# A random-feature attention with a feed-forward part: weight loads in turns of five, a key chunk's two loads asked for together, the second tile's attention behind a gate

## The chip, the cores and the metric

The kernel runs on one core of a Trainium2 chip. Its time is the device time of one execution in microseconds (us). The engines are PE (TensorE), DVE (VectorE), ACT (ScalarE), POOL (GpSimd) and SP (SyncE), which here issues all the transfers. "Before" is the kernel as it was, "after" the one with the change.

## The reference

```python
# q, k, v: (8, 8, 576, 64); omega: (128, 64); x: (8, 576, 512); w_ch1: (512, 2048); w_ch2: (2048, 512)
def phi(x):
    proj = np.einsum('bhsd,md->bhsm', x, omega)
    sq = np.sum(x * x, axis=-1, keepdims=True) / 2.0
    h = proj - sq
    h = h - np.max(h, axis=-1, keepdims=True)
    return np.exp(h) / np.sqrt(m)
q_p, k_p = phi(q * scale), phi(k * scale)
kv = np.einsum('bhsm,bhsd->bhmd', k_p, v)
z = np.sum(k_p, axis=2)
num = np.einsum('bhsm,bhmd->bhsd', q_p, kv)
den = np.einsum('bhsm,bhm->bhs', q_p, z)[..., None] + 1e-06
x = (num / den) with the heads side by side
xn = (x - mean) / np.sqrt(var + 1e-06) * g_ln
out = x + np.maximum(xn @ w_ch1, 0.0) @ w_ch2
```

Everything is 32-bit. A batch's `kv` needs all 576 of its keys, so no query of a batch gets its numerator before the batch's last key chunk is through.

## The kernel before, in words

**Stages.** Attention goes by key chunks and query blocks. A batch has five key chunks (four of 128 rows, one of 64): keys and values are loaded (L372, L376), projected on PE (L439), reduced to row maxima on DVE (L395), put through the exponential on ACT (L401), multiplied with the values on PE (L418), and added up in `kv` on DVE (L424). A query block has 256 rows, loaded in two parts (L465), projected (L494), copied out of PSUM by ACT or DVE (L229, L231), reduced over partitions on POOL (L478), subtracted on DVE (L480) and exponentiated on ACT (L483). For each 128 rows `gen_x` multiplies with `kv` (L555), divides, and takes the norm's statistics; `gen_xnT` normalizes and transposes (L624, L628, L630) into `xnT`, of which there is one.

The feed-forward part takes the 4608 rows as nine tiles of 512. A tile has 16 steps f. A step is `mm1` (L651 to L653, twelve matmuls of 128x512), a relu on ACT and DVE (L662, L664) and `mm2` (L684 to L686, twelve matmuls). A tile begins when its four transposed chunks and the first four w1 parts are there.

**Weights.** Each of w1 and w2 comes in 16 parts of 512 KB as 64-bit words that hold doubles. `gen_w` loads a part (L314) into a tile of its own and turns it, by six operations on ACT and DVE (L321 to L354), into two 32-bit parts in place, the rounded value and the rest. At most three are converted at once (`turn_w`). `mm1` at step f needs w1 parts up to the end of f's group of four, `mm2` needs w2 part f. The converted weights stay for the whole kernel.

**The order of the work.** Every piece is a Python generator that asks a planner for names (`get`: a tile, a PSUM bank, or a mere turn that stands for no memory), for engine time (`run`, with an assumed cost) or for another piece's result (`wait`). The planner simulates the engines with its assumed costs and emits instructions in the order that comes out: among what could start first on an engine, the lowest rank goes. That order is fixed in the program; on the chip each engine, SP too, takes its instructions in order and waits for data by semaphores. Ranks: a batch's keys start at `NS * (b * S // T) + RK`, a block's queries at `NS * (blk * QB // T) + RQ + 4 * (blk % 2)`, with NS = 32, RK = -30, RQ = -22, so -30 and -22 for the first tile and 2 and 10 for the second; weights at `RW0 + RW * f` (w1) and one more (w2), from -12 and -11 to 18 and 19; the feed-forward part comes behind all of them on PE, and its relu ahead of all of them on ACT and DVE. While no feed-forward matmul has started, `gen_warm` fills PE's planned idle time with small matmuls (L709), whose result is not used.

Names of which there are few: 15 wide tiles for raw keys, queries, query features, conversions and normalized rows (`wide`, N_BIG); two key turns; two query turns; two blocks at once; three value tiles.

In `gen_keys` the values of a chunk are asked for when its keys have landed, by the planner's clock, and the next chunk's keys when the values have:

```python
                yield dma(P * NP * r)
                nc.sync.dma_start(kraw, kT[b, c] if c < NFULL else kTr[b])
                t_v = yield "get", n_v
                v = tile_of(t_v, [P, H, D + 1])
                yield dma(P * H * D)
                nc.sync.dma_start(v[0:r], vF[b, c] if c < NFULL else vR[b])
```

Of the kernel before, what the change touches and what calls it, by code (L numbers as in the profile page):

```python
# [12 lines left out]
F32 = mybir.dt.float32  # L13
BF16 = mybir.dt.bfloat16
F32R = mybir.dt.float32r
U32 = mybir.dt.uint32
# [6 lines left out]
P = 128  # L23
B, H, S, D = 8, 8, 576, 64
M = 128
DM = H * D
DFF = 4 * DM
NP = H // 2
NK = DM // P
NF = DFF // P  # L30
NFULL = S // P
# [4 lines left out]
T = 512  # L36
# [3 lines left out]
QB = 256  # L40
# [28 lines left out]
class Plan:  # L69
# [73 lines left out]
    def free(self, *names):  # L143
        for n in names:
            assert n not in self.places, n
            self.places[n] = self.cur.seen()
            self.cur.holds -= n[0] == "b" and 0 < self.cur.holds
            self.wake(lambda w: w[0] == "get" and n in w[1])

    def done(self, key):  # L150
        self.made[key] = self.cur.seen()
        self.wake(lambda w: w == ("wait", key))
# [38 lines left out]
def favor_ffn(ctx, tc, kT, kTr, vF, vR, qT, omT, gT, w1, w2, out):  # L191
# [12 lines left out]
    nc = tc.nc  # L204
    const = ctx.enter_context(tc.tile_pool(name="const", bufs=1))
    wp = ctx.enter_context(tc.tile_pool(name="wp", bufs=1))
    sb = ctx.enter_context(tc.tile_pool(name="sb", bufs=1))
    ps = ctx.enter_context(tc.tile_pool(name="ps", bufs=1, space=PSUM))
    plan = Plan()
    free, done = plan.free, plan.done  # L210

    def f32(ap):
        return ap.bitcast(F32)
# [4 lines left out]
    def dve(n, k=1, c=0.065):  # L218
        return "run", {DVE: k * (c + 0.00105 * n)}
# [4 lines left out]
    def dma(n):  # L224
        return "run", {SP: n * 4e-6 / 0.36}

    def copy(eng, out, in_):
        if eng == ACT:
            nc.scalar.copy(out=out, in_=in_)  # L229
        else:  # L230
            nc.vector.tensor_copy(out, in_)  # L231

    def scaled(eng, out, in_, c):
        if eng == ACT:
            nc.scalar.activation(out=out, in_=in_, func=AF.Copy, scale=c)
        else:
            nc.vector.tensor_scalar(out=out, in0=in_, scalar1=c, scalar2=None, op0=ALU.mult)

    def wait(*key):
        return "wait", key  # L240

    def names(tag, n):
        return plan.own(*(f"{tag}{i}" for i in range(n)))

    def tile_of(tag, shape, dtype=F32, pool=sb):
        return pool.tile(shape, dtype, tag=tag, name=tag, bufs=1)

    def bank(tag, n=512):
        return tile_of(tag, [P, 512], F32, ps)[:, 0:n]


    n_big, n_x, n_kp, n_v, n_kv = names("wide", N_BIG), names("x", 9), names("kp", 2), names("v", 3), names("kv", 3)
    n_hid, n_xnT, n_mb, n_st = names("hid", 2), names("xnT", 1), names("mb", 3), names("st", 9)
    turn = {k: names(f"turn_{k}", n) for k, n in (("k", 2), ("q", 2), ("blk", 2), ("mx", 2), ("xn", 4), ("w", 3))}
    n_w = {(n, f): names(f"w{n}_{f}", 1) for f in range(NF) for n in (1, 2)}
    banks = names("b", 8)
    b_at, b_h, b_acc = banks[0:2], banks[2:4], banks[4:8]
# [14 lines left out]
    nc.vector.memset(eps, EPS)  # L272
    g_sb = const.tile([P, NK], F32, name="g_sb")
    om_raw = tile_of("hid0", [P, M])
    if TILED:
        om = const.tile([P, M], F32, name="om")
# [31 lines left out]
    wparts = {}  # L308

    def gen_w(n, f):  # L310
        tag = yield "get", n_w[n, f]
        yield dma(2 * P * DM)
        r = tile_of(tag, [P, DM, 2], U32, wp)
        nc.sync.dma_start(r.rearrange("p a b -> p (a b)"), (w1, w2)[n - 1][f])  # L314
        w_turn = yield "get", turn["w"]
        wt = yield "get", n_big
        eng = yield "run", {ACT: 0.56, DVE: 0.34}
        t = tile_of(wt, [P, DM], U32)
        sign = 0x80000000
        if eng == ACT:  # L320
            nc.scalar.activation(out=t, in_=r[:, :, 0], func=AF.Copy, scale=2.0**-29 * 7.49 / 8)  # L321
            yield dve(DM)
            nc.vector.scalar_tensor_tensor(
                out=r[:, :, 0], in0=r[:, :, 1], scalar=sign, in1=t, op0=ALU.bitwise_and, op1=ALU.bitwise_or
            )
            eng = yield "run", {ACT: 0.56, DVE: 0.34}
            scaled(eng, f32(r[:, :, 1]), f32(r[:, :, 1]), 2.0**-112)
        else:
            nc.vector.tensor_scalar(out=t, in0=r[:, :, 1], scalar1=sign, scalar2=None, op0=ALU.bitwise_and)
            eng = yield "run", {ACT: 0.56, DVE: 0.34}  # L330
            scaled(eng, f32(r[:, :, 1]), f32(r[:, :, 1]), 2.0**-112)
            yield dve(DM)
            nc.vector.scalar_tensor_tensor(
                out=r[:, :, 0], in0=r[:, :, 0], scalar=29, in1=t, op0=ALU.logical_shift_right, op1=ALU.bitwise_or
            )
        yield dve(DM)
        nc.vector.scalar_tensor_tensor(  # L337
            out=t, in0=r[:, :, 1], scalar=3, in1=r[:, :, 0], op0=ALU.logical_shift_left, op1=ALU.bitwise_or
        )
        if n == 1:  # L340
            yield wait("g")
        eng = yield "run", {ACT: 0.56, DVE: 0.34}
        w = wparts[n, f] = tile_of(tag, [P, 2, DM], F32R, wp)
        if n == 1:
            g = g_sb[:, f % NK : f % NK + 1]
            scaled(eng, w[:, 0], f32(t), g)
            yield dve(DM)
            nc.vector.scalar_tensor_tensor(
                out=w[:, 1], in0=f32(t), scalar=g, in1=f32(w[:, 0]), op0=ALU.mult, op1=ALU.subtract
            )  # L350
        else:
            copy(eng, w[:, 0], f32(t))
            yield dve(DM)
            nc.vector.tensor_tensor(out=w[:, 1], in0=f32(t), in1=f32(w[:, 0]), op=ALU.subtract)  # L354
        free(wt, w_turn)
        done(("w", n, f))

    kvs, phis, xs, xnTs = {}, {}, {}, {}
# [1 line left out]

    def gen_keys():
        for b in range(B):
            t_kv = yield "get", n_kv
            kvs[b] = t_kv, tile_of(t_kv, [P, H, D + 1])
            for c in range(NFULL + 1):
                plan.cur.rank = NS * (b * S // T) + RK + 2 * c
                r = P if c < NFULL else REM
                k_turn = yield "get", turn["k"]
                t_k = yield "get", n_big
                kraw = tile_of(t_k, [P, NP, r])  # L370
                yield dma(P * NP * r)
                nc.sync.dma_start(kraw, kT[b, c] if c < NFULL else kTr[b])  # L372
                t_v = yield "get", n_v
                v = tile_of(t_v, [P, H, D + 1])
                yield dma(P * H * D)
                nc.sync.dma_start(v[0:r], vF[b, c] if c < NFULL else vR[b])  # L376
                t_kp = yield "get", n_kp
                t_mb = yield "get", n_mb
                plan.add(plan.cur.rank, gen_k(b, c, r, kraw, v, (t_k, k_turn), (t_kp, t_mb, t_v)))
# [131 lines left out]

    def gen_queries():
        for blk in range(NB):
            plan.cur.rank = NS * (blk * QB // T) + RQ + 4 * (blk % 2)
            b_turn = yield "get", turn["blk"]
            plan.add(plan.cur.rank, gen_block(blk, b_turn))

    def gen_block(blk, b_turn):
        rank = plan.cur.rank
        for j in range(2):  # L520
            plan.add(rank, gen_q(blk, j))
        for i in range(2):
            plan.add(rank + 6 + 2 * i, gen_x(2 * blk + i))
        for j in range(2):
            for s in range(2):
                yield wait("phi", blk, j, s)
        yield wait("num", 2 * blk)
        yield wait("num", 2 * blk + 1)
        free(*(phis[blk, j, s][0] for j in range(2) for s in range(2)), b_turn)
# [203 lines left out]
    NS = 2 * NF  # L733
    plan.add(-300, gen_const())
    for f in range(NF):
        plan.add(RW0 + RW * f, gen_w(1, f))
        plan.add(RW0 + RW * f + 1, gen_w(2, f))
    plan.add(RK, gen_keys())
    plan.add(RQ, gen_queries())
    plan.add(URGENT, gen_xnT())  # L740
    for b in range(B):
# [5 lines left out]

TILED = True
N_BIG = 15
WARM, COLD = 0.1, 5.0  # L750
RW0, RW = -12, 2
RK, RQ = -30, -22


# [32 lines left out]
```

## Time and profile before

| | |
|---|---|
| time, median of 3 runs | 1142.06 us (1141.39 to 1143.84) |
| the profiled execution: time, span | 1141.77 us, 1139.9 us |
| mean granted clock of PE | 0.974 |
| busy: PE, DVE, ACT, POOL | 1100.3, 484.8, 330.2, 131.2 us |
| moved by DMA | 55.70 MB |
| first feed-forward matmul (L651) starts | 132.07 us |
| weight loads (L314) | 32 of 512 KB, 2.6 to 42.4 us, median 9.4 us from issue to landing |

Busy time counts when an engine has an instruction under way. Matmuls are pipelined, so PE's filler matmuls and its useful ones both count as busy, and a busy PE is not PE at its peak. A row of a group reads: line, engine, operation, output and input, shapes and count, then busy time, mean length in ns, and the idle time ahead of it with what ended it. SPq is SP's queue, which issues transfers. Clock and DMA lines on the page stand for 40 equal slices of the span, in tenths.

### The profile page before, as it was taken

How to read it: one execution, taken by the hardware profiler on the slowest of the kernel's cores; microseconds unless marked ns; L12 is line 12 of the kernel's file. 1: busy time of each engine (PE TensorE's matmuls, PEld its weight loads, DVE VectorE, ACT ScalarE, POOL GpSimd, SP SyncE). 2: the span in 40 equal slices, each digit the busy share in tenths (PEclk: the TensorE clock that was granted, in tenths of full speed). 3: DMA queues.
4: the chain of work that ended last, by engine and by line, in shares of the span. 5: the costliest groups of instructions: out<-in, count | busy, mean ns of one | idle time of the engine just before them, and what ended most of it. 6: DMA issues, size and time to landing. Idle time of an engine off the chain costs nothing.

```text
span 1139.9 us, 15141 instructions
## 1 busy us (share of the span) xinstructions
PE 1100.3 (97%) x6135; PEld 902.2 (79%) x6135; DVE 484.8 (43%) x1074; ACT 330.2 (29%) x795; POOL 131.2 (12%) x77
## 2 busy tenths in 40 slices
PE   5669999999999999999999999999999999999998
PEld 3558888788788878887888788887887888888886
DVE  3997844534741373136422642164137116113111
ACT  3884623343331134113321242123113112111110
POOL 2200500400400050004000220013004000000000
PEclk8776999999999999999999999999999999999999
DMA  9802212012100120003100310020011000000000
GB/s 355 330 28 84 66 56 59 28 56 93 47 1 1 46 92 22 1 4 127 28 1 1 112 43 6 1 74 1 1 38 38 1 1 37 1 1 37 1 1 37
DMA packets 26340, 55.70 MB, mean 49 GB/s; under 512 B 3104, under 2 KB 4256, under 8 KB 26272
## 3 DMA queue, kind: packets, MB, share of 16 engines
q1 hardware_dynamic: 26272, 54.75, 13.9%
q8 instruction: 48, 0.79, 0.3%
q14 instruction: 20, 0.16, 0.0%
HBM read 45.30 MB, written 9.44 MB: 48 GB/s over the span
## 4 chain that ended last, share of the span: by engine, by line
PE 90%; DVE 5%; ACT 2%; DMA 1%; issue 1%; POOL 0%; SPq 0%; DVEq 0%
PE b L651 12%; PE b L684 12%; PE b L686 12%; PE b L685 12%; PE b L653 11%; PE b L652 11%; PE b L418 6%; PE b L555 6%; PE b L439 4%; PE b L494 3%; PE b L624 1%; DVE wide L337 1%; DMA w<-w 1%; DVE w L354 1%; ACT kp L401 1%
## 5 line engine op out<-in xcount | busy, mean ns | idle before, releaser
L664 DVE SCALAR_TENSOR_TENSOR hid<-b,hid 128x512 fp32r<-128x512 f32 x144 | 99.5, 691 | 464.4 <-ACT hid L662 464.2
L662 ACT ACTIVATE hid<-b 128x512 fp32r<-128x512 f32 x144 | 86.2, 599 | 519.5 <-PE b L653 519.3
L684 PE MATMUL b<-w,hid 128*128 128x512 f32 x576 | 233.7, 406 | 0.1
L651 PE MATMUL b<-xnT,w 128*128 128x512 f32 x576 | 232.9, 404 | 0.0
L686 PE MATMUL b<-w,hid 128*128 128x512 f32 x576 | 226.5, 393 | 0.0
L685 PE MATMUL b<-w,hid 128*128 128x512 f32 x576 | 226.0, 392 | 0.0
L653 PE MATMUL b<-xnT,w 128*128 128x512 f32 x576 | 225.2, 391 | 0.0
L652 PE MATMUL b<-xnT,w 128*128 128x512 f32 x576 | 224.7, 390 | 0.0
L478 POOL PARTITION_ALL_REDUCE wide<-wide x72 | 130.8, 1889 | 741.3 <-ACT wide L229 634.8
L651 PEld LDWEIGHTS b<-xnT,w 128*128 128x128 f32 x576 | 108.3, 188 | 29.4 <-issue 7.5
L684 PEld LDWEIGHTS b<-w,hid 128*128 128x128 f32 x576 | 108.2, 188 | 26.4 <-issue 3.0
L686 PEld LDWEIGHTS b<-w,hid 128*128 128x128 f32 x576 | 108.1, 188 | 24.6
L653 PEld LDWEIGHTS b<-xnT,w 128*128 128x128 f32 x576 | 108.1, 188 | 23.5
L685 PEld LDWEIGHTS b<-w,hid 128*128 128x128 f32 x576 | 108.4, 188 | 21.4
L652 PEld LDWEIGHTS b<-xnT,w 128*128 128x128 f32 x576 | 108.4, 188 | 20.0
L418 PE MATMUL b<-v,kp 128*128 128x65 f32 (+1 forms) x640 | 85.2, 284 | 30.6 <-ACT kp L401 30.2
L418 PEld LDWEIGHTS b<-v,kp 128*128 128x128 f32 (+1 forms) x640 | 83.7, 201 | 38.7 <-ACT kp L401 32.2
L401 ACT ACTIVATE kp<-b,mb 128x128 f32<-128x128 f32 (+1 forms) x320 | 87.5, 382 | 74.2 <-DVE mb L395 74.2
L555 PEld LDWEIGHTS b<-kv,wide 128*128 128x128 f32 (+1 forms) x640 | 72.9, 195 | 6.5 <-issue 2.6
L480 DVE TENSOR_TENSOR wide<-wide,wide 128x512 f32<-128x512 f32 x72 | 69.5, 976 | 18.1 <-POOL wide L478 18.0
L555 PE MATMUL b<-kv,wide 128*128 128x65 f32 (+1 forms) x640 | 72.5, 276 | 1.9 <-DVE st L561 1.7
L395 DVE TENSOR_REDUCE mb<-b 128x4 f32<-128x512 f32 (+1 forms) x80 | 51.8, 684 | 40.4 <-PE b L439 40.3
(51 smaller groups left out, 745.2 us busy)
## 6 DMA issues: line engine op xcount, KB each, us to landing
w<-w SPq DMA_DIRECT2D x32, 512.0 KB, 9.4
wide<-qT SPq DMA_DIRECT2D x36, 256.0 KB, 3.1
out<-x SPq DMA_DIRECT2D x36, 256.0 KB, 2.1
v<-vF SPq DMA_DIRECT2D x32, 260.0 KB, 2.9
wide<-kT SPq DMA_DIRECT2D x32, 256.0 KB, 2.9
v<-vR SPq DMA_DIRECT2D x8, 130.0 KB, 2.6
wide<-kTr SPq DMA_DIRECT2D x8, 128.0 KB, 2.6
hid<-omT SPq DMA_DIRECT2D x1, 64.0 KB, 1.8
```

Source lines behind the costliest of these rows:

```text
L401: nc.scalar.activation(out=kp[0:r, j], in_=pk[0:r, i], func=AF.Exp, scale=1.0, bias=mb[0:r, j : j + 1])
L418: nc.tensor.matmul(pv[:, i], kp[0:r, slot(h)], v[0:r, h], start=True, stop=True)
L478: nc.gpsimd.partition_all_reduce(mx, qc, P, bass_isa.ReduceOp.max)
L555: nc.tensor.matmul(pn[a:z, i], phi(blk, h, slice(cols + a, cols + z)), kvs[b][1][:, h], start=True, stop=True)
L651: nc.tensor.matmul(ph, w[:, 0, cs], xnT[:, 0, k], start=(k == 0), stop=False)
L652: nc.tensor.matmul(ph, w[:, 1, cs], xnT[:, 0, k], start=False, stop=False)
L653: nc.tensor.matmul(ph, w[:, 0, cs], xnT[:, 1, k], start=False, stop=(k == NK - 1))
L662: nc.scalar.activation(out=hl[:, 0], in_=ph, func=AF.Relu)
L664: nc.vector.scalar_tensor_tensor(out=hl[:, 1], in0=ph, scalar=0.0, in1=f32(hl[:, 0]), op0=ALU.max, op1=ALU.subtract)
L684: nc.tensor.matmul(accs[i], hl[:, 0, cs], w[:, 0], start=(f == 0), stop=False)
L685: nc.tensor.matmul(accs[i], hl[:, 0, cs], w[:, 1], start=False, stop=False)
L686: nc.tensor.matmul(accs[i], hl[:, 1, cs], w[:, 0], start=False, stop=(f == NF - 1))
```

## The change

Five edits, none of which changes what is computed or how much of it:

- A weight part must hold one of five load turns (`turn_wl`) from ahead of its load until it is converted.
- A key chunk's keys and values are asked for in one step of the planner, with the keys' size counted twice.
- The second batch's keys wait until w2 part 7 is converted, the third query block (the first of the second tile) until w2 part 8 is: that is nine parts of w2, 0 to 8.
- The weights' ranks become -14 + f for w1 and -5 + f for w2.
- `tile_of` picks the weights' pool by the tile's name, where `gen_w` named it.

```diff
-    turn = {k: names(f"turn_{k}", n) for k, n in (("k", 2), ("q", 2), ("blk", 2), ("mx", 2), ("xn", 4), ("w", 3))}
+    turn = {k: names(f"turn_{k}", n) for k, n in (("k", 2), ("q", 2), ("blk", 2), ("mx", 2), ("xn", 4), ("w", 3), ("wl", 5))}
...
-    def tile_of(tag, shape, dtype=F32, pool=sb):
+    def tile_of(tag, shape, dtype=F32, pool=None):
+        pool = pool or (wp if tag[1].isdigit() and tag[0] == "w" else sb)
...
     def gen_w(n, f):
+        load_turn = yield "get", turn["wl"]
         tag = yield "get", n_w[n, f]
         yield dma(2 * P * DM)
-        r = tile_of(tag, [P, DM, 2], U32, wp)
+        r = tile_of(tag, [P, DM, 2], U32)
...
-        free(wt, w_turn)
+        free(wt, w_turn, load_turn)
         done(("w", n, f))
...
     def gen_keys():
         for b in range(B):
+            if b == 1:
+                yield wait("w", 2, GATE_K)
...
-                yield dma(P * NP * r)
-                nc.sync.dma_start(kraw, kT[b, c] if c < NFULL else kTr[b])
                 t_v = yield "get", n_v
                 v = tile_of(t_v, [P, H, D + 1])
-                yield dma(P * H * D)
+                yield dma(2 * P * NP * r)
+                nc.sync.dma_start(kraw, kT[b, c] if c < NFULL else kTr[b])
                 nc.sync.dma_start(v[0:r], vF[b, c] if c < NFULL else vR[b])
...
     def gen_queries():
         for blk in range(NB):
+            if blk == T // QB:
+                yield wait("w", 2, GATE_Q)
...
-        plan.add(RW0 + RW * f, gen_w(1, f))
-        plan.add(RW0 + RW * f + 1, gen_w(2, f))
+        plan.add(RW1 + RS * f, gen_w(1, f))
+        plan.add(RW2 + RS * f, gen_w(2, f))
...
+GATE_K, GATE_Q = 7, 8
-RW0, RW = -12, 2
+RW1, RW2, RS = -14, -5, 1
```

More of the change, by code (lines that the diff above doesn't have):

```diff
@@ L342, in gen_w @@
         eng = yield "run", {ACT: 0.56, DVE: 0.34}
-        w = wparts[n, f] = tile_of(tag, [P, 2, DM], F32R, wp)
+        w = wparts[n, f] = tile_of(tag, [P, 2, DM], F32R)
         if n == 1:
```

## The prediction

> **What bounds the kernel now.** I read the page first, then a table of the span cut where the first matmul of the feed-forward part (L651) starts, then the order of events ahead of that point.
>
> ```profile
> span 1139.9 us, 15141 instructions
> ...
> DVE  3997844534741373136422642164137116113111
> ...
> PEclk8776999999999999999999999999999999999999
> DMA  9802212012100120003100310020011000000000
> ```
>
> DVE is full and PE's clock below full speed only in the first slices, and DMA is busy only there. The cut table (columns: PE, PEld, DVE, ACT, POOL busy with counts, granted clock, DMA share, GB/s):
>
> ```profile
> 0.00:132.07 132.07, 98.33 (x711) 82.27 (x711) 104.36 (x216) 82.46 (x177) 23.53 (x18) 0.78 0.48 180
> 132.07:1139.90 1007.83, 1001.97 (x5426) 819.91 (x5425) 380.45 (x859) 247.69 (x618) 107.71 (x60) 1.00 0.10 32
> ```
>
> From 132.07 us on PE works 1001.97 of 1007.83 us at full clock. Nothing but less PE work could shorten that stretch, and the change removes none. The first 132 us are different. PE's groups there, by line:
>
> ```profile
> L709 PE MATMUL b<-spin 128*128 128x256 bf16 x326 | 44.7, 298 | 1.2 <-DVE spin L265 1.2
> L418 PE MATMUL b<-v,kp 128*128 128x65 f32 (+1 forms) x112 | 19.8, 339 | 30.2 <-ACT kp L401 30.2
> ...
> L439 PE MATMUL b<-om,wide 64*128 64x128 f32 (+1 forms) x128 | 11.4, 328 | 0.0
> L494 PE MATMUL b<-wide,om 64*128 64x256 f32 x64 | 9.8, 429 | 2.0 <-DMA wide<-qT 2.0
> ```
>
> 44.7 us of "busy" is the warm-up filler of L709, which computes nothing, and 30.2 us are idle behind ACT's exponentials. So the bound is the start of the feed-forward part. What sets it is in the order of events (start, length, engine):
>
> ```profile
> 11.01 0.44 SPq L372 DMA_DIRECT2D wide<-kT  x1
> ...
> 12.20 16.26 SPq L314 DMA_DIRECT2D w<-w  x14
> ...
> 18.76 7.41 POOL L478 PARTITION_ALL_REDUCE wide<-wide  x4 [9.70 <-issue]
> 20.60 1.56 DVE L480 TENSOR_TENSOR wide<-wide,wide 128x512 f32<-128x512 f32 x1 [9.80 <-POOL wide L478]
> ...
> 29.35 0.33 SPq L376 DMA_DIRECT2D v<-vF  x1
> ...
> 30.59 12.11 SPq L314 DMA_DIRECT2D w<-w  x11
> ...
> 43.73 0.33 SPq L372 DMA_DIRECT2D wide<-kT  x1
> ...
> 44.55 1.16 PE L439 MATMUL b<-om,wide 64*128 64x128 f32 x16
> ...
> 73.18 1.16 PE L439 MATMUL b<-om,wide 64*128 64x128 f32 x16
> ...
> 86.91 2.08 PE L439 MATMUL b<-om,wide 64*128 64x128 f32 x16
> ...
> 94.02 1.09 PE L439 MATMUL b<-om,wide 64*64 64x128 f32 x16
> ```
>
> The second key chunk's keys are issued at 11.01, its values at 29.35, with weight loads between; the third chunk's keys at 43.73, behind the last weight load. The first batch's chunks 1 to 4 reach PE at 44.55, 73.18, 86.91 and 94.02. Only then can the first tile's numerators (L555) start, as the chain of waits shows (start, length):
>
> ```profile
> 101.17 13.92 PE b L555 x64
> 115.09 2.01 PE b L439 x16
> ...
> 117.64 1.40 PE b L439 x16
> ...
> 121.78 1.03 ACT kp L401 x4
> 122.90 1.03 ACT kp L401 x4
> ...
> 124.41 1.05 ACT kp L401 x4
> 125.50 2.00 PE b L418 x16
> ...
> 128.38 1.73 PE b L418 x16
> 130.12 1.09 PE b L439 x16
> 131.21 0.87 PE b L494 x8
> 132.07 0.43 PE b L651
> ...
> 132.75 0.23 PE b L653
> ```
>
> L439, L418, L401 and L494 after 115 us belong to the second tile: five first-batch chunks and two query blocks were already through. They sit ahead of the first tile's last transposes.
>
> **The change part by part.** *Key and value loads together.* Each chunk loses one serial wait, in which the values were asked for only after the keys had landed. SP issues the same DMAs; their place among the weight loads changes. *Five load turns.* `turn_wl` is a name in the planner and no tile, so the chip gets no new semaphore from it: it changes the emitted order. A load is put behind key loads that have become due, and the fourteen and eleven weight loads in a row disappear. A first-tile chunk should then meet a few weights ahead of it, not all 32. The pool choice in `tile_of` gives the same tiles: nothing. *Ranks.* w1 goes ahead of w2; the order from the ranks is five loads in order of asking (w1 0, w2 0, w1 1, w2 1, w1 2), then w1 3 to 10, and from there w2 2 and on alternating. *Gates.* The second batch's keys wait for w2 7, which by that order is about the 24th weight of 32, the third query block for w2 8, about the 25th. In the emitted order this moves L439, L418, L494 and all their ACT, DVE, POOL and SP instructions behind those conversions; behind the waiting generator only later batches are queued.
>
> *Where the start goes.* DVE cannot go on before 20.60, since the first all-reduce began at 18.76 after 9.70 us of issue; the change doesn't touch that, so I keep it. In a sentence that the sum doesn't use: the Trainium skill (GPSIMD Engine Reference, 2.1 Instruction dispatch) gives about 6 us for the first call of a freshly loaded routine; by it DVE would be let go 3.7 us sooner and the time would be 1090. The row's 9.70 is longer, and decides.
>
> From 20.60, chunk by chunk: with keys and values in time the shortest spacing seen is 94.02 - 86.91 = 7.1 us, and that with DVE full of conversions. Four more chunks make 28.4, the last kv add about 1 (an estimate): L555 starts at 50. From L555 to L651 took 132.07 - 101.17 = 30.9 us. The second tile's pieces quoted above (2.01 + 1.40 + 3.11 + 3.73 + 1.09 + 0.87 = 12.2) leave by the gate: 18.7. So the feed-forward part starts at **69 us** (20.6 + 28.4 + 1 + 18.7).
>
> The same from DVE's work, since DVE may be what is full:
>
> ```profile
> L337 DVE SCALAR_TENSOR_TENSOR wide<-w 128x512 uint32<-128x512 uint32 x32 | 22.5, 717 | 0.0
> L323 DVE SCALAR_TENSOR_TENSOR w<-w,wide 128x512 uint32<-128x512 uint32 x27 | 18.5, 694 | 0.5 <-ACT wide L321 0.5
> L348 DVE SCALAR_TENSOR_TENSOR w<-wide,g_sb,w 128x512 fp32r<-128x512 f32 x16 | 12.0, 749 | 0.0
> L354 DVE TENSOR_TENSOR w<-wide,w 128x512 fp32r<-128x512 f32 x16 | 11.9, 743 | 0.0
> ```
>
> These four groups are 64.9 us for 32 weights, 2.03 us of DVE each. DVE worked 104.36 us before 132.07, so some 39 us were attention; by the chunks and blocks that stay behind the gate about a quarter of that goes (an estimate), leaving 29. With N weights converted ahead of the start, it comes at 20.6 + 29 + 2.03 N. Ten weights give 70, in agreement; the six that are needed or asked first give 62, sixteen give 82. I take 69, with 50 (chunks at 2.5 us each: 20.6 + 10 + 1 + 18.7) and 85 (seventeen weights between) as ends.
>
> Clock: the chain's L555 took 13.92 us for 64, while the granted clock was about half:
>
> ```profile
> 100.00:110.00 10.00, 9.76 (x50) 9.39 (x49) 6.90 (x22) 2.46 (x5) 0.00 (x0) 0.56 0.25 69
> 110.00:120.00 10.00, 10.00 (x68) 8.86 (x68) 6.97 (x33) 0.87 (x5) 0.00 (x0) 0.59 0.20 65
> ```
>
> The same work in the changed kernel also follows gaps at ACT's exponentials, so I keep 13.92; at twice the clock it would be 7 us shorter, inside my lower end. The Trainium skill (TensorE: Matmul & The Clock Gate, Part 1) says full clock comes after about 3.4 us of sustained activity, which would end the half clock early in L555 and bring the time to about 1089. Here PE was busy 19.76 of 20 us and stayed near half, so this trace speaks against it.
>
> *What the later part gets back.* Ahead of 132.07 the old kernel had also done second-tile work: 128 - 80 = 48 records of L439 (three chunks), 112 - 80 = 32 of L418 (two chunks), 64 - 32 = 32 of L494 (four groups of 8). At full clock that is 3 x 1.09 + 2 x 1.73 + 4 x 0.87 = 10.2 us; each return to the feed-forward part costs 0.43 - 0.23 = 0.2, nine times 1.8. Sum 12.0 us, now behind the start.
>
> *New waits in the first tile.* Weights must now arrive while PE uses them. A step f is 24 matmuls at 0.23, 5.5 us; 16 steps are 88 us for the 22 weights left, 4.0 us each, against 2.03 of DVE. Where weights and relu (L662, L664) stand in a line on ACT and DVE, PE can still wait some tenths per step: 0 to 15 us, and I take 3, near the lower end because DVE needs only half of its time. Below nothing is excluded: no PE work disappears.
>
> **Sum.** 69 + 1007.8 + 12.0 + 3 = 1091.8 us of span. The profiled execution took 1141.77 for 1139.9 of span, 1.9 more: 1093.7, or **1094 us**. That execution is 0.3 below the median of 1142.06, too little to matter.
>
> **The rivals.** *Weights too late.* The start comes early, but PE waits for weights. For: they are now loaded and converted under the feed-forward part, with relu on the same two engines. Against: the 2.03 us. It decides when a weight takes more than 4.0 us; at 5 us each, 22 take 110 instead of 88, and the time is 1094 + 22 = 1116.
>
> *The second tile too late, the one that ends slower.* The gate holds the second batch's keys until about weight 24. PE has 88 us of steps and about 26 us of the second tile's attention (as the first tile's: 5 x 1.09 + 5 x 1.73 + 4 x 0.87, half of 13.92 for L555 and, an estimate, 2 for L624) until 69 + 88 + 26 = 183. At 2.5 us per weight (32 in the 80 us from 20 to 100) the gate opens at 69 + 14 x 2.5 = 104; five chunks at 7.1 and 31 us of the rest end at 171, in time. At the mean spacing of before, (94.02 - 44.55) / 3 = 16.5, they end at 104 + 82 + 31 = 217, a gap of 34 us and 1128. It turns the result slower once the second tile is ready after 183 + 48 = 231, that is a gate at 118 with the old spacing; at 4 us per weight it opens at 125, and the time is 1149.
>
> *The order doesn't really change.* The five turns bind only the planner, and DVE was full from 20 to 100 us. If nearly all 32 conversions still go ahead of the first tile's last steps, the start is 20.6 + 29 + 65 = 115, and 115 + 12 + 1007.8 + 3 + 1.9 gives 1140, no change. Against: the planner gives a free engine to the lowest rank that is ready, and the keys' ranks (-30 to -22) are below the weights'; it was the loads that were missing.
>
> **How the numbers follow.** Start between 55 and 85: 0.70. Earlier still: 0.07, about 1075. Weights late: 0.10. Second tile late enough to be slower: 0.08. Order unchanged: 0.05, of which 0.04 within 0.2% (2.3 us, about what a measurement of this kernel can tell from no change) and 0.01 faster. Faster is 0.70 + 0.07 + 0.10 + 0.01 = 0.88, same 0.04, slower 0.08. The low end is a start at 50 without new waits, 50 + 1007.8 + 12 + 1.9 = 1072; the high end a start at 85 with about 13 us of new waits, 1120. What lies outside is most of the slower case, the unchanged order and the tails.
>
> **What would show it.** In the profile after: the first batch's five key loads issued before about 30 us with weights between; the L439 rows of chunks 1 to 4 by 50; L651 first at 55 to 85 and far fewer L709 records than 326; the conversions (L337) running on beside L651; no second-batch L439 ahead of the first L651; and PE at 99% afterwards. A first L651 past 100, idle PE between L653 and L684 behind a weight's L354, or a gap of PE ahead of the second tile's first L651 would make it wrong, each by one of the rivals.

## The result, and the profile after

After the change the kernel takes 1111.7 us (median of 4 runs, 1108.05 to 1113.58) against 1141.72 for the kernel before: ratio 0.9733, 95% interval 0.970 to 0.9765. The gain is 30 us; 48 was forecast, with a range of 1072 to 1120. The profiled execution took 1110.21 us for a span of 1108.4.

The page of the kernel after, the lines that answer to those of before:

```profile
span 1108.4 us, 14732 instructions
...
DVE  4889746456446542274216531471165125113111
...
PEclk8689998999999999999999999999999999999999
DMA  6735111301202110031003100200020001001001
```

DVE is about as full in the first slices as before; PE's clock stands at nine tenths from the fourth slice (but for the seventh) and not from the fifth, and what DMA moves is spread out. The table cut at the first matmul of the feed-forward part (now L656; the lines have moved by up to five), with the columns of before:

```profile
0.00:72.64 72.64, 58.31 (x399) 49.51 (x399) 51.82 (x126) 37.56 (x93) 16.02 (x13) 0.77 0.66 251
72.64:1108.40 1035.76, 1027.42 (x5537) 830.91 (x5536) 434.21 (x953) 290.00 (x699) 113.70 (x64) 1.00 0.11 36
```

The start came 59.4 us sooner, and the rest became 27.9 us longer. PE's groups ahead of the start:

```profile
L714 PE MATMUL b<-spin 128*128 128x256 bf16 x126 | 21.5, 332 | 1.2 <-DVE spin L266 1.2
L560 PE MATMUL b<-kv,wide 128*128 128x65 f32 x64 | 13.1, 403 | 0.0
L421 PE MATMUL b<-v,kp 128*128 128x65 f32 (+1 forms) x80 | 11.7, 305 | 9.7 <-ACT kp L404 9.7
L442 PE MATMUL b<-om,wide 64*128 64x128 f32 (+1 forms) x80 | 8.0, 358 | 0.0
L497 PE MATMUL b<-wide,om 64*128 64x256 f32 x32 | 4.2, 388 | 1.3 <-DMA wide<-qT 1.3
```

There are exactly the 80, 80 and 32 records of the first tile, and 126 of the filler against 326. The order of events on SP, POOL, DVE and PE:

```profile
5.30 0.43 SPq L378 DMA_DIRECT2D wide<-kT  x1
...
10.26 0.45 SPq L378 DMA_DIRECT2D wide<-kT  x1
...
12.60 0.33 SPq L378 DMA_DIRECT2D wide<-kT  x1
...
34.24 0.33 SPq L378 DMA_DIRECT2D wide<-kTr  x1
...
18.13 7.69 POOL L481 PARTITION_ALL_REDUCE wide<-wide  x4 [9.28 <-DMA w<-w]
19.97 1.55 DVE L483 TENSOR_TENSOR wide<-wide,wide 128x512 f32<-128x512 f32 x1 [8.02 <-POOL wide L481]
...
12.85 1.16 PE L442 MATMUL b<-om,wide 64*128 64x128 f32 x16
32.09 2.08 PE L442 MATMUL b<-om,wide 64*128 64x128 f32 x16
36.35 1.86 PE L442 MATMUL b<-om,wide 64*128 64x128 f32 x16
40.53 1.09 PE L442 MATMUL b<-om,wide 64*64 64x128 f32 x16
```

The third chunk's keys are asked for at 10.26 instead of 43.73, and chunks 1 to 4 reach PE by 40.53 instead of 94.02. That the start came sooner is what was forecast. What was not forecast is on the page too, in the groups of the feed-forward matmuls over the whole execution. Before:

```profile
L651 PE MATMUL b<-xnT,w 128*128 128x512 f32 x576 | 232.9, 404 | 0.0
...
L653 PE MATMUL b<-xnT,w 128*128 128x512 f32 x576 | 225.2, 391 | 0.0
L652 PE MATMUL b<-xnT,w 128*128 128x512 f32 x576 | 224.7, 390 | 0.0
```

After:

```profile
L656 PE MATMUL b<-xnT,w 128*128 128x512 f32 x576 | 236.8, 411 | 0.0
...
L658 PE MATMUL b<-xnT,w 128*128 128x512 f32 x576 | 228.3, 396 | 0.4 <-DVE xnT L635 0.3
L657 PE MATMUL b<-xnT,w 128*128 128x512 f32 x576 | 228.2, 396 | 0.0
```

The same matmuls of the first product are 7, 5 and 6 ns longer, 576 times each: 10.4 us. The second product takes 2.2 us more in all. In the last tile, where nothing else runs, starts in the first product are 227 ns apart before and 232 to 235 after (medians by line over the trace's records). The 27.9 us are then 10.4 from this; 12.9 of moved work (48 records of L442, 32 of L421 and 32 of L497 more than before, 10.5 us by their spacing, and 12 more returns to the feed-forward part at 0.2); and some 4.6 left, for the second product and for new waits.

### The profile page after: what moved, and what is told of

Same layout as the page of the kernel before. It is cut to its first block, busy times and chain, and to the rows that moved or that the text cites. A ratio compares the mean times of both kernels' runs of the same rounds, so it can differ in the third digit from the quotient of the medians.

```text
span 1108.4 us, 14732 instructions
## 1 busy us (share of the span) xinstructions
PE 1085.7 (98%) x5934; PEld 880.4 (79%) x5934; DVE 486.0 (44%) x1078; ACT 327.6 (30%) x791; POOL 129.7 (12%) x77
## 4 chain that ended last, share of the span: by engine, by line
PE 94%; DVE 2%; DMA 2%; ACT 1%; SPq 0%; issue 0%; POOL 0%; POOLq 0%; ACTq 0%
PE b L656 13%; PE b L689 13%; PE b L658 12%; PE b L657 12%; PE b L690 12%; PE b L691 12%; PE b L421 6%; PE b L560 6%; PE b L442 4%; PE b L497 3%; PE b L629 1%; PE b L714 1%; DMA wide<-kT 1%; DMA w<-w 1%; ACT kp L404 1%
## 5 line engine op out<-in xcount | busy, mean ns | idle before, releaser
L656 PE MATMUL b<-xnT,w 128*128 128x512 f32 x576 | 236.8, 411 | 0.0
L658 PE MATMUL b<-xnT,w 128*128 128x512 f32 x576 | 228.3, 396 | 0.4 <-DVE xnT L635 0.3
L657 PE MATMUL b<-xnT,w 128*128 128x512 f32 x576 | 228.2, 396 | 0.0
L656 PEld LDWEIGHTS b<-xnT,w 128*128 128x128 f32 x576 | 108.6, 189 | 32.0 <-issue 8.3
L689 PEld LDWEIGHTS b<-w,hid 128*128 128x128 f32 x576 | 108.4, 188 | 27.9 <-issue 3.5
L691 PEld LDWEIGHTS b<-w,hid 128*128 128x128 f32 x576 | 108.2, 188 | 25.2
L421 PEld LDWEIGHTS b<-v,kp 128*128 128x128 f32 (+1 forms) x640 | 80.5, 194 | 17.4 <-ACT kp L404 10.2
L421 PE MATMUL b<-v,kp 128*128 128x65 f32 (+1 forms) x640 | 81.0, 276 | 9.7 <-ACT kp L404 9.7
L560 PEld LDWEIGHTS b<-kv,wide 128*128 128x128 f32 (+1 forms) x640 | 74.2, 197 | 8.1 <-issue 4.5
L560 PE MATMUL b<-kv,wide 128*128 128x65 f32 (+1 forms) x640 | 73.6, 278 | 3.1 <-DVE st L566 1.7
```

The lines of the kernel that those rows point to most:

```text
L421: nc.tensor.matmul(pv[:, i], kp[0:r, slot(h)], v[0:r, h], start=True, stop=True)
L560: nc.tensor.matmul(pn[a:z, i], phi(blk, h, slice(cols + a, cols + z)), kvs[b][1][:, h], start=True, stop=True)
L656: nc.tensor.matmul(ph, w[:, 0, cs], xnT[:, 0, k], start=(k == 0), stop=False)
L657: nc.tensor.matmul(ph, w[:, 1, cs], xnT[:, 0, k], start=False, stop=False)
L658: nc.tensor.matmul(ph, w[:, 0, cs], xnT[:, 1, k], start=False, stop=(k == NK - 1))
L689: nc.tensor.matmul(accs[i], hl[:, 0, cs], w[:, 0], start=(f == 0), stop=False)
```

## The experiments

All times are compared with the kernel before on the same chip. Two theories were to be told apart for each open point: why the first product became slower, what holds the start at 72 us, and which of the edits carries the gain.

**Why the first product is slower.** The new order changes the order in which tiles are first made, and so their places. In the program as built, `xnT` starts at byte 195072 of a partition before, a multiple of 512, and at 192992 after, which is a multiple of 32 only. Two pads of unused bytes move it, and three kernels test it.

```diff
                 if i == 0:
                     t_t = yield "get", n_xnT
+                    if t == 0:
+                        tile_of("pad0", [P, 8])
                     xnTs[t] = t_t, tile_of(t_t, [P, 2, NK, T], F32R)
+                    if t == 0:
+                        tile_of("pad1", [P, 8])
```

First, this edit in the kernel after.

> The kernel after, with 32 unused bytes ahead of xnT and 32 behind it, so that xnT starts at byte 193024 of a partition (a multiple of 64) in place of 192992 (a multiple of 32 only); everything else lies 64 bytes further, and the order is the same. Theory A (the place of xnT slows mm1): the spacing of matmuls in the first product falls from 233 to 227 ns, 1728 of them give 10 us, so the ratio to before goes from 0.973 to about 0.964 (1101 us). Theory B (another chip, or the new order, or the weights' new places slow them): no change, 1110 us and 233 ns.

Measured: 1098.8 us, ratio 0.963 (0.9607 to 0.9653). The groups of the first product, in a window of the last tiles (1000 to 1070 us), after and with the pads:

```profile
L658 PE MATMUL b<-xnT,w 128*128 128x512 f32 x51 | 20.2, 396 | 0.0
L656 PE MATMUL b<-xnT,w 128*128 128x512 f32 x50 | 19.8, 396 | 0.0
L657 PE MATMUL b<-xnT,w 128*128 128x512 f32 x50 | 19.8, 396 | 0.0
```

```profile
L660 PE MATMUL b<-xnT,w 128*128 128x512 f32 x55 | 21.4, 390 | 0.0
L662 PE MATMUL b<-xnT,w 128*128 128x512 f32 x54 | 21.1, 390 | 0.0
L661 PE MATMUL b<-xnT,w 128*128 128x512 f32 x54 | 21.0, 389 | 0.0
```

Second, the same edit in the kernel before.

> The kernel before, with the same two pads: xnT moves from 195072 (a multiple of 64) to 195104 (a multiple of 32 only). Theory A: the first product's matmuls go from 227 to 233 ns apart, and the time rises by about 10 us to 1152 (ratio 1.009). Theory B: no change, ratio 1.000.

Measured: 1153.14 us, ratio 1.0093 (1.0076 to 1.0111), with 395 ns in the same window:

```profile
L655 PE MATMUL b<-xnT,w 128*128 128x512 f32 x49 | 19.4, 395 | 0.0
L657 PE MATMUL b<-xnT,w 128*128 128x512 f32 x49 | 19.4, 395 | 0.0
L656 PE MATMUL b<-xnT,w 128*128 128x512 f32 x49 | 19.3, 395 | 0.0
```

Third, the control: `[P, 16]` in pad0 and no pad1.

> The control for the first: the kernel after with 64 unused bytes ahead of xnT and none behind, so that all tiles lie where they do in the first experiment, but xnT is again a multiple of 32 only (193056). Theory A: 233 ns and 1110 us as after. Theory B, in the form that the shift of the other tiles matters: the same time as the first experiment.

Measured: 1106.02 us, ratio 0.9664 (0.9638 to 0.969), 234 ns between starts in the first product. The spacing is theory A's; the time is 4 us better than expected. It is still 7 us above the first experiment, whose tiles differ from it in the place of `xnT` alone, though single executions of the two overlap (1099.43 to 1107.04 against 1094.52 to 1104.34), so that the spacing is what decides here. Moving `xnT` by 32 bytes thus costs or saves some 10 us in either kernel and either direction, with no instruction changed: theory A holds. All the good places of `xnT` were multiples of 512. The traces hold another place, however: the moving operand of the second product is a w2 part, and every w2 part starts 256 bytes above a multiple of 512. Those matmuls start 227 ns apart where the other operand lies well (the twelfth experiment below), so 256 is as good as 512, and what is open lies between 32 and 256 bytes.

**What holds the start.** POOL's first all-reduce starts at 18.13 us although its input is there sooner. Its row above puts the wait down to a weight's DMA, but the all-reduce reads no weight. Ahead of it stands the select that makes the identity:

```profile
8.57 0.28 POOL L269 TENSOR_SCALAR_AFFINE_SELECT ident<-ident 128x128 f32<-128x128 f32 x1 [8.15 <-DVE mb L398]
```

In the trace's records a pair of MODIFY_POOL_CONFIG stands ahead of `affine_select` (0.9 us) and another ahead of the first all-reduce (9.1 us). So the identity, needed only by the transposes at 64 us, seems to cost a load of code ahead of the one that matters. The fourth kernel has the pads of the first and this:

```diff
-    nc.gpsimd.affine_select(
-        out=ident, in_=ident, compare_op=ALU.not_equal, fill=1.0, base=0, pattern=[[-1, P]], channel_multiplier=1
-    )
+    reduces = []
...
             nc.gpsimd.partition_all_reduce(mx, qc, P, bass_isa.ReduceOp.max)
+            reduces.append(0)
+            if len(reduces) == 8:
+                nc.gpsimd.affine_select(
+                    out=ident, in_=ident, compare_op=ALU.not_equal, fill=1.0, base=0, pattern=[[-1, P]], channel_multiplier=1
+                )
```

> The first experiment's kernel, with POOL's affine_select that makes the identity moved behind the eighth partition_all_reduce, so behind the first tile's queries. Theory C (POOL's first all-reduce waits for two loads of code one after the other, first that of affine_select): the first all-reduce starts at about 10 instead of 18 us, DVE no longer stands idle for 8 us, L560 starts some 8 us sooner, and the time is 6 to 9 us below the first experiment. Rival D (the code load waits for the DMA engines, full until 22 us, or the start is set by something else such as the key loads): the first all-reduce still starts at 17 to 18 us, or the first feed-forward matmul still at about 72, and the time is that of the first experiment.

Measured: 1084.32 us, ratio 0.9488 (0.9471 to 0.9506). POOL, the first numerators and the start:

```profile
8.77 8.00 POOL L479 PARTITION_ALL_REDUCE wide<-wide  x4 [8.34 <-DVE wide L231]
...
38.38 7.26 PE L563 MATMUL b<-kv,wide 128*128 128x65 f32 x64
...
57.74 0.50 PE L663 MATMUL b<-xnT,w 128*128 128x512 f32 x1
```

The first experiment has the numerators at 47.08 and the start at 66.77, so both come 9 us sooner: theory C. That the select ahead of the all-reduce costs these 9 us is shown. That what passes in them is a load of code is read from the MODIFY_POOL_CONFIG records: in this kernel one pair stands ahead of the all-reduce, at 0.8 us, and the late select has none and runs at once, in 0.43 us at 31.16. The time fell by 14, more than expected; between the two profiled executions it is 1092.8 - 1082.3 = 10.5 us of span. The rest lies in the other runs of the first experiment, whose mean granted clock is 0.979 to 0.983, against 0.989 in its profiled one and 0.993 to 0.996 here. In that experiment the time goes with the clock (1094.52 us at 0.989, 1104.34 at 0.979); why the clock is steadier with the late select is not shown.

The clock also moves the start by itself. The order of the first experiment is that of the kernel after, and its numerators begin at the same time, but they ran at full clock:

```profile
47.08 7.26 PE L560 MATMUL b<-kv,wide 128*128 128x65 f32 x64
```

7.26 us instead of 13.1, and the start 66.77 instead of 72.64. A half-clock stretch fell on 48.1 to 65.2 us in the one execution; in the other there was only a short one there, from 58.6 to 62.0.

The eleventh experiment is the late `affine_select` alone, in the kernel before.

> The kernel before with the late affine_select alone; xnT stays at a multiple of 64. Theory (in the kernel before, the key loads behind the weights set the start, and in the planned order DVE has enough other work): POOL's first all-reduce at about 9 us, but the first feed-forward matmul not more than 3 us earlier, ratio 0.997 to 1.000. Rival (DVE's amount of work sets it): the start comes 7 to 10 us earlier, ratio 0.991 to 0.994.

Measured: 1132.49 us, ratio 0.9929 (0.9908 to 0.995), all-reduce and start at

```profile
7.54 7.80 POOL L476 PARTITION_ALL_REDUCE wide<-wide  x4 [7.11 <-ACT wide L229]
...
120.87 0.50 PE L654 MATMUL b<-xnT,w 128*128 128x512 f32 x1
```

The start came 11.1 us sooner (132.00 in the same view before): the rival holds, and the theory falls. The late key loads had shaped the planned order, but on the chip DVE was full with that order (9.4 to 10.0 us of every ten from 20 to 80 us), and what delayed DVE ahead of that went through to the start. The rows of before agree: the third chunk's keys, asked for at 43.73 us, were projected only at 73.18, where a key load lands 2.9 us after its issue (median).

**Which edit carries the gain.** Four kernels, all with `xnT` at a multiple of 512 (three by themselves, the seventh by the pads), so that the first experiment (0.963) is the twin, not the kernel after. The twin is exact for the seventh alone: the other three differ from it in the place of `hid1`, too, which is worth some 5 us to them (twelfth experiment).

The fifth drops the two `yield wait("w", 2, GATE_...)`.

> The kernel after without its two gates; xnT lies at a multiple of 64 bytes by itself (195072), so it is compared with the first experiment (ratio 0.963, first feed-forward matmul at 67 us). Theory (the gates only move second-tile work between two places where PE has it to do anyway): the start comes up to 12 us later, the rest is shorter by the same, and the time stays within 5 us of the first experiment's 1099. Rival (the gates are needed, since second-tile work takes DVE from the first tile and from the weights): start past 85 us, 1110 us or more.

Measured: 1094.26 us, ratio 0.9599 (0.9546 to 0.9653). It started at 83.07, 16 us later, and its rest of the span is 1092.0 - 83.07 = 1008.9 against 1092.8 - 66.77 = 1026.0. The start is later than the 12 us that were expected. The second-tile work went to the other side of the start and nothing was gained or lost that the interval shows: the theory holds for the time. With the place of `hid1` taken off, the gates may still be worth a few us, which this interval cannot show.

The sixth drops `load_turn`.

```diff
-        load_turn = yield "get", turn["wl"]
...
-        free(wt, w_turn, load_turn)
+        free(wt, w_turn)
```

> The kernel after without the five load turns, all else as after; xnT at a multiple of 64 by itself, compared with the first experiment. Theory (the order of loads is the cause: without turns all 32 weights are asked for at once and the third chunk's keys again stand behind most of them): the third chunk's keys issued after 30 us, first feed-forward matmul at 80 to 95 us, 1112 to 1127 us. Rival (ranks, gates and the joint load are enough): start within 5 us of 67, 1099 us.

Measured: 1130.12 us, ratio 0.9887 (0.9854 to 0.9921). SP's queue:

```profile
11.32 6.75 SPq L315 DMA_DIRECT2D w<-w  x6
18.41 0.33 SPq L377 DMA_DIRECT2D wide<-kT  x1
20.28 22.77 SPq L315 DMA_DIRECT2D w<-w  x20
44.01 0.33 SPq L377 DMA_DIRECT2D wide<-kT  x1
```

The chunk that is caught behind the weights is the fourth and not the third, twenty loads in a row come back, and the start is at 114.4, later than expected. The rival falls clearly.

The seventh asks for values after keys again.

```diff
+                yield dma(P * NP * r)
+                nc.sync.dma_start(kraw, kT[b, c] if c < NFULL else kTr[b])
                 t_v = yield "get", n_v
                 v = tile_of(t_v, [P, H, D + 1])
-                yield dma(2 * P * NP * r)
-                nc.sync.dma_start(kraw, kT[b, c] if c < NFULL else kTr[b])
+                yield dma(P * H * D)
```

> The kernel after with keys and values asked for one after the other as before, turns, ranks and gates kept, padded so that xnT is a multiple of 64; compared with the first experiment. Theory (each of four chunks gets one more wait for a landing behind up to five weights, 3 to 4.5 us): L560 starts 12 to 18 us later, 1110 to 1117 us. Rival (DVE's work, not the loads, spaces the chunks once the weights are held back): no change, 1099 us.

Measured: 1116.79 us, ratio 0.9763 (0.9739 to 0.9788). The start is at 88.06, and the first numerators stand at 67.81 instead of 47.08:

```profile
67.81 7.26 PE L561 MATMUL b<-kv,wide 128*128 128x65 f32 x64
```

The theory holds, with 21 us in place of 12 to 18.

The eighth is the kernel before with the joint load and the turns alone.

> The kernel before with only the joint load and the five turns, old ranks and no gates; xnT at a multiple of 64. Theory (these two edits carry the gain, ranks and gates little): first numerators by 60 us, 1099 to 1110 us. Rival (the old ranks with no gates let second-tile work and w2 in ahead): start past 95 us, 1120 us or more.

Measured: 1091.38 us, ratio 0.9547 (0.9531 to 0.9563), better than expected and better than the kernel after. Its first numerators come at 47.14 us, as early as with all five edits:

```profile
47.14 2.79 PE L555 MATMUL b<-kv,wide 128*128 128x65 f32 x24
```

Joint load and turns carry the gain, and the whole of it needs both: without the turns 0.9887, without the joint load 0.9763.

**Why the eighth beats the first.** In the fifth, sixth and eighth kernels the second product too is faster, 227 ns between starts against 229 to 234 in the others. There `hid1` lies at 211456, a multiple of 512; before, after and in the padded kernels it is a multiple of 32. The ninth kernel is the fourth with `[P, 16]` in pad1, which puts `hid1` at 209472, a multiple of 64.

> The fourth experiment's kernel (after, affine_select late, xnT at a multiple of 64) with 32 more unused bytes behind xnT, so that hid1 too lies at a multiple of 64 bytes (209472 in place of 209440). Theory (the weight side of a matmul is slowed by such a place too, since the three kernels with hid1 at a multiple of 64 show 227 ns between matmuls of the second product and the others 229 to 232): the second product goes to 227 ns, 5 to 7 us less, 1078 us (ratio 0.943). Rival (those three kernels differ in something else): 230 ns and 1084 us.

Measured: 1087.55 us, ratio 0.9531 (0.9476 to 0.9587), 231 ns. The theory falls as it was put: 64 bytes do not help. The twelfth drops pad1, so that `hid1` is at 209408, a multiple of 512.

> The ninth experiment's kernel without the bytes behind xnT, so that hid1 lies at 209408, a multiple of 512 bytes as xnT does, and not at a multiple of 64 alone (209472). Theory (the place of hid1 slows the second product, and 64 is too fine a grid: the fast kernels had it at 211456, a multiple of 512): 227 ns between matmuls of the second product in place of 231, 5 to 7 us less than the fourth experiment, 1078 us, ratio 0.943 to 0.945. Rival (the 227 ns of the four kernels comes from something else, such as the weights' places or the distance to hid0): 230 ns, 1084 us.

Measured: 1080.64 us, ratio 0.947 (0.9456 to 0.9483). The second product's groups in the window of the last tiles, the fourth kernel and the twelfth:

```profile
L698 PE MATMUL b<-w,hid 128*128 128x512 f32 x52 | 20.4, 393 | 0.0
L697 PE MATMUL b<-w,hid 128*128 128x512 f32 x52 | 20.4, 392 | 0.0
L696 PE MATMUL b<-w,hid 128*128 128x512 f32 x52 | 20.4, 392 | 0.0
```

```profile
L695 PE MATMUL b<-w,hid 128*128 128x512 f32 x53 | 20.6, 389 | 0.0
L696 PE MATMUL b<-w,hid 128*128 128x512 f32 x53 | 20.6, 389 | 0.0
L694 PE MATMUL b<-w,hid 128*128 128x512 f32 x53 | 20.6, 389 | 0.0
```

3 to 4 ns go, 227 between starts as in the first product, and the span of the profiled execution falls by 1082.3 - 1077.3 = 5 us. So the operand that is loaded as weights has a place that counts, too, and its grid is coarser than 64 bytes. The traces say more when the steps of the second product are parted by the tile that they use. `hid0` lies at 132864 in every kernel, 256 bytes above a multiple of 512. Over the last 300 us, starts with `hid0` are 227 ns apart (median) in the fourth, ninth and twelfth kernels alike, and those with `hid1` 232, 235 and 227: the whole difference is in the steps of `hid1`, and 256 is as good as 512. Whether 128 is enough stays open. Where `xnT` lies badly (after, second and third kernels) the steps with `hid0` are at 228 to 231, though both of their operands lie 256 bytes above a multiple of 512 there, too; why is open. The medians' difference (1084.3 to 1080.6, on two chips) is smaller than the 5 to 7 us expected, and the two intervals just overlap.

The tenth is the eighth with the late `affine_select`.

> The kernel before with the joint load, the five turns and the late affine_select, without gates and new ranks; both tiles at multiples of 64 by themselves. It is the ninth experiment's kernel without ranks and gates. Theory (ranks and gates are worth nothing once the loads come in time): within 4 us of the ninth experiment, 1075 to 1082 us. Rival (they matter when the start comes earlier): 5 us or more above it.

Measured: 1083.04 us, ratio 0.95 (0.9454 to 0.9546). It was to be compared with the ninth, and is 4.5 us below that one; but with `hid1` at 211456 its true twin is the twelfth, and the two cannot be told apart. Ranks and gates are worth nothing here that these runs can show. The twelfth kernel, with all five edits, beats both kernels: 1080.6 against 1111.7 and 1141.8.

## Why the prediction was right, and which term was mis-sized

**The bound and its mover were right.** The start of the feed-forward part set the time, and the joint load with the turns brought it forward (sixth, seventh and eighth experiments). That the key loads behind the weights had made it late holds for the planned order; on the chip the chain before went through DVE's work in that order (eleventh experiment).

**The loads.** The runs of fourteen and eleven weight loads were to disappear. Ahead of the fifth chunk's keys, which are asked for at 34.24 us where about 30 was named, only seven weights are asked for, one or two at a time. Behind them a longer run came than any before:

```profile
35.26 22.61 SPq L316 DMA_DIRECT2D w<-w  x21
```

It held up no keys and no queries of the first tile, since all of these had been asked for.

**The start** was put at 69 and came at 72.6. Its terms are off in opposite directions. The chunks: L560 was to start at 50 and started at 47.42, as chunks 2 to 4 follow each other at 4.2 us and not 7.1. The rest: 18.7 us were kept, and it took 25.2, as conversions (L339, L350, L325) now stand between the first tile's last DVE steps, seven of them from 64.5 us to the start, 4.9 us in all. DVE's own sum, with ten weights, was close: nine L339 lie ahead of the start.

**The clock** was taken at half for L555, and the trace was said to speak against the Trainium skill's rule (TensorE: Matmul & The Clock Gate, Part 1). Both clocks occur: L560 took 13.1 us after, where PE was busy for all of 50 to 60 us at a clock of 0.50, and 7.26 in the first experiment, same order. It is a difference between executions of about 6 us, not a constant of the kernel.

**POOL's wait** was kept at 9.70 us because the change does not touch it. That was right for the forecast. It was not a fixed cost, though: it goes when the select no longer stands ahead of the all-reduce (fourth and eleventh experiments), and by the records the second load of code begins only when the select is through. The Trainium skill's figure of about 6 us (GPSIMD Engine Reference, 2.1 Instruction dispatch) is for one load; here the two took 7.7 us (0.9 to 8.6) and 9.0 us (9.1 to 18.1).

**The moved work** was 12.0 us and measured 12.9, with the very counts of matmuls that were forecast; the returns were twelve more and not nine.

**The new waits in the first tile** were put at 3 us for weights and relu. No wait of PE for a weight is in the profile: from the start to 170 us PE is busy 97.03 of 97.36.

```profile
72.64:170.00 97.36, 97.03 (x520) 76.94 (x519) 71.98 (x127) 60.28 (x125) 11.28 (x7) 1.00 0.24 74
```

What there is comes at the second tile's numerators, PE's wait for a bank that DVE has yet to empty, and a few us of half clock behind it:

```profile
173.58 1.21 PE L560 MATMUL b<-kv,wide 128*128 128x65 f32 x8 [1.46 <-DVE x L570]
174.55 0.78 PE L656 MATMUL b<-xnT,w 128*128 128x512 f32 x1
```

A matmul of L656 takes 0.78 us there in place of 0.50. The half-clock stretch is 6.8 us long and so costs about 3.4; with the 1.46 that is 4.9, about the 4.6 left over. The split is an estimate: the 2.2 us of the second product are in the 4.6 as well, and a part of the half-clock time is in the 10.4 of the first product.

**The step that failed** is the base of the sum, "Nothing but less PE work could shorten that stretch, and the change removes none", with the 1007.8 us carried over unchanged. It was mis-sized by 10.4 us (9.7 by the first experiment, which with `xnT` moved back needs 1026.0 us from its start on in place of 1035.8). An edit that alters the order alters the places of the tiles, and PE's rate depends on those (first three experiments). Start 3.6, moved work 0.9, places 10.4 and waits with the second product about 1.7 more than the forecast make 16.6, the difference between a span of 1091.8 and 1108.4.

**The rivals.** Weights too late: no. Second tile too late: no. Its first projection came at 113.83 with the gate forecast at 104, and its numerators at 170.07 with 171 forecast for the case in time. The order unchanged: no, but the eleventh experiment shows that DVE's work was the chain on the chip before, as that rival said.

## What to carry to other kernels

A change of order is also a change of places: where an engine-bound stretch gets slower per instruction with the same instructions, compare the start addresses of its operands before looking for waits. Loads that can wait should be limited by what consumes them, and loads that belong together asked for in one step, so that a planner's queue does not put bulk ahead of a chain. Look at what an engine does with its first microseconds: a constant that is needed late can hold up a routine that is needed early.

## What the runs showed of the hardware that was not expected

- The start address of a matmul's moving operand counted: 227 ns between 128x512 matmuls with `xnT` at multiples of 512 bytes (195072, 193024), 232 to 235 at odd multiples of 32 (192992, 195104, 193056). In the second product it was 227 ns with the w2 parts 256 bytes above a multiple of 512. The Trainium skill (SBUF — State Buffer, Operand start alignment) asks for no more than the element size, 4 bytes here, and says that this is about what is allowed and not about speed; these runs give the speed.
- The start address of the operand that is loaded as weights counted as well: 227 ns with `hid1` at 211456 or 209408, 229 to 234 at 213536, 213600, 209440, 209376 and 209472, the last a multiple of 64. Half of the second product's steps use `hid1`, and these medians are over all steps; its own steps were 232 ns apart at 209440, 235 at 209472 and 227 at 209408, those of `hid0` at 132864 (256 above a multiple of 512) 227 in the same three executions.
- POOL's first all-reduce started at 18.13 us with `affine_select` ahead of it and at 8.77 without.
- The granted clock in the first 70 us differed between executions of the same order: L560's 64 matmuls took 13.1 us or 7.26.
